# Four pairs' down rows stored plainly and added later, weight tails stored once, and the second half's operands prepared one name a gap

## The chip, the cores and the metric

The kernel runs on one core of a Trainium2 chip. Its time is the device time of one execution in microseconds (us). Times below come from three runs and from one further execution that was taken with the hardware profiler. The engines are TensorE (PE; PEld is its weight load), VectorE (DVE), ScalarE (ACT), GpSimd (POOL) and SyncE (SP, which here only issues DMAs). Sixteen DMA engines move the data of all queues.

## The reference

```python
x = A_x                                             # (1, 2048, 576); B_x is drawn too, but not read here
g = sigmoid((x * gate_w).sum(-1, keepdims=True))
a = irfft2(rfft2(x, axes=(-2, -1)) * (w_r + 1j * w_i), s=(2048, 576), axes=(-2, -1))
h = gelu(x @ w_gate, tanh approximation) * (x @ w_up)   # 576 -> 4608
b = h @ w_down                                      # 4608 -> 576
return g * a + (1 - g) * b
```

All is float32. The kernel splits an operand of a matmul into a high and a low part and adds the products of high with high, low with high and high with low, so one logical matmul is three or more.

## The kernel before

**Tiling.** The 2048 tokens are two halves of 1024 (p = 0, 1), the 4608 hidden features 36 tiles of 128, taken in 18 pairs i. The first two pairs of the first half are done in `normal`; all other work comes in 34 groups `(p, i)`: pairs 2 to 17 of the first half, then 0 to 17 of the second. A group is one call of `products`.

**A group.** Gate and up products of a group are formed from seven products of sums and differences of blocks (the names a11, a12, s2, s3, s1, a22, s4). Each product is `seven`, called for two column halves: six 128x512 matmuls on the 512 main features and a seventh (L1367) on the *tail*. The tail is the 32 features a half has left over. Its operand has 128 rows: on the weight side the high part of the 32 rows twice and the rest twice, on the x side high, rest, high, rest, so that one matmul forms all four cross products. Between the products stand the matmuls of `down` for earlier groups (L963): they multiply by `w_down` into a PSUM tile `pdn`, ACT drains it to one of four `stg` buffers (L995), and `put` sends `stg` to the DRAM buffer `yd[u]` of its 128 tokens, u = 0 to 15: the first time plainly from SP, later with an accumulating DMA from POOL (L976).

**Weight tails.** The tails of a pair's weights are worked out once, from the input `wt`, by `tail_piece`, ten times: `load` (L1242), `total` (four subtractions, L1246), `high` (a copy), `rest` (L1253) and `store` to the DRAM buffer `tails_d` (L1260). The first two pieces run before the first group, the other eight in the first groups, each spread over gaps 1 to 11 of every 12. They work in `wtb`: `raw_t` its first 896 columns, `high_t` its last 896. Before each product, `prep` loads its tail from DRAM into a weight slot (L1344), a DMA of 128 KB, three products ahead. There are four slots.

**What sets the order.** The program is written out in order by Python code. A *gap* is a point between matmuls at which `gap()` issues what is due: functions put there by `at(n, fn)`, n gaps ahead, and then steps of generators as long as their `credit` lasts, which grows with PE's work. The engines run their own instructions strictly in that order; SP and POOL queue DMAs in that order, and an instruction that waits holds all behind it on its engine.

**The spectral part** runs as such a generator beside the products, mostly on DVE and ACT: row transforms of each half of the tokens, then `columns` (column products on PE, L349, whose frequency-dependent factors come by DMA from POOL and SP), the inverse, and `adds`, which adds the result into `yd` by accumulating DMAs from POOL (L710). `inverse_rows(0)` and `(1)` do that for the two halves. In the last group `load_last` loads `yd[8..15]` back (L1017) for the last down rows.

**The second half's operands.** `other_operands` runs in the first half's groups near their end. It takes blocks of x of the second half (three at a time in `quads`), forms sums, and for each of seven names a high and a low part, which it stores to `kept_*` in DRAM (L1181, L1174). At the turn from the first to the second half, `swap` loads them.

The tail's load and store before, and the tail operand's copy:

```python
d = tails_d[n].rearrange("(r q p) k -> q r p k", r=4, q=4)          # prep, L1343
nc.sync.dma_start(f(w[:, 512:768]), d[q, :, :, 256 * m:256 * (m + 1)])
for r, x in enumerate((f(high_t), f(high_t), raw_t, raw_t)):         # store, L1259
    nc.sync.dma_start(d[r, 0:w, n % 2], x[0:w])
for q in (0, 64):                                                    # tail_of, L1053
    copy(o[q:q + 32], x[q:q + 32])
```

Of the kernel before, what the change touches and what calls it, by code (L numbers as in the profile page):

```python
# [10 lines left out]
F32 = mybir.dt.float32  # L11
# [4 lines left out]
P = 128  # L16
# [143 lines left out]
def _build(nc, tc, a):  # L160
    with ExitStack() as ctx:
# [34 lines left out]
        def set_tmp():  # L196
# [18 lines left out]
        tails_d = [dram.tile([4 * P, 7 * 256], F32, name=f"tails{i}", tag=f"tails{i}") for i in range(len(PAIRS))]  # L215
        yd = [dram.tile([P, D], F32, name=f"yd{i}", tag=f"yd{i}") for i in range(NB)]

        def ps_gu():
# [69 lines left out]
        def columns():  # L288
# [129 lines left out]
            for kb in range(16):  # L418
                was, more = kb > 0, kb + 1 < 16
                v = product(0, kb, xh, xl)  # L420
                if was:
                    copy(yh, vs)
                yield from step()
                copy(zr, v[:, 1, :NK])
                copy(t0, v[:, 0, :NK])
                yield from step()
                if was:
                    vec.tensor_tensor(yl, vs, f(yh), ALU.subtract)
                vec.tensor_tensor(zi, t0, zr, ALU.subtract)
# [24 lines left out]
                yield from waits(STEP - 7)  # L454
# [203 lines left out]
        def inverse_rows(h):  # L658
# [93 lines left out]
        added = {}  # L752
        aux = []
        later = []
        gens = []
        side = []
        credit = [0.0]
# [13 lines left out]
            later.sort(key=lambda x: x[0])  # L771

        def gap():

            count[0] += 1
            while later and later[0][0] <= count[0]:
                later.pop(0)[1]()
            if aux:
                aux.pop(0)()
            credit[0] = min(credit[0], cap[0])  # L780
            if not gens:
                return
            ahead = side and ops.get("ahead")
            while ahead and credit[0] > 0:
                v = next(side[0], None)
                if v is None:
                    break
                credit[0] -= v
            while credit[0] > 0:
                try:  # L790
                    v = next(gens[0])
                except StopIteration:
                    gens.pop(0)
                    v = None
                if v is None:
                    while side and not ahead and credit[0] > 0:
                        v = next(side[0], None)
                        if v is None:
                            break
                        credit[0] -= v  # L800
                    return
                credit[0] -= v
# [161 lines left out]
                          start=part == 0 and n == 0, stop=part == 1 and n == 2)  # L964
            tick(6 * 0.131)

        def put(u, write, first):

            o = stg[dnn[0] % 4].rearrange("p c k -> p (c k)")
            dnn[0] += 1  # L970
            added[u] = count[0]
            write(o)
            if first:
                nc.sync.dma_start(yd[u], o)
            else:
                pl.dma_start(yd[u], o, accum_op=ALU.add)  # L976

        def down(prev, t):
# [12 lines left out]
                copy(held(u).rearrange("p (c k) -> p c k", c=2), v[:, :, 0:HD])  # L991
            else:
                assert ops.get('released', 0) > min(dnn[0], 3)
                n = 1 if ops.get("late") else 0
                at(n, lambda: put(u, lambda o: act.activation(o.rearrange("p (c k) -> p c k", c=2), v[:, :, 0:HD], AF.Copy,  # L995
                                                              scale=omg[:, u:u + 1]), i == 0))
            behind[0] = t % 2 == 0
            gap()
            behind[0] = False
# [47 lines left out]
        def tail_of(o, x):  # L1047
# [98 lines left out]
        def other_operands():  # L1146
# [6 lines left out]
                ring.append(ring.pop(0))  # L1153
                return ring[-1]

            def highs(names, i):
                q = quads[i]
                at_ = dict(a11=q[0], a12=q[1], a22=q[3], s1=q[3], s3=q[2], s2=q[0], s4=q[1])
                out = []
                for n in names:  # L1160
                    out.append((n, i, at_[n], place()))
                    copy(fr(out[-1][3]), out[-1][2])
                return out

            def rests(items):
                for n, i, x, h in items:
                    o = h if i == 2 else x if n[0] == "s" else place()
                    vec.tensor_tensor(fr(o), x, h, ALU.subtract)
                    if i == 2:
                        def turn(h=h, x=x):  # L1170
                            for q in (0, 64):
                                copy(fr(h[q:q + 32]), x[q:q + 32])
                        at(1, turn)
                        at(2, lambda n=n, h=h: nc.sync.dma_start(kept[n][:, 2048:], h))  # L1174
                        yield 0.72
                        yield None
                        continue
                    else:
                        def store(n=n, i=i, h=h, o=o):
                            for c, s in ((0, h), (1, o)):  # L1180
                                nc.sync.dma_start(kept[n][:, 1024 * c + TB * i:1024 * c + TB * (i + 1)], s)  # L1181
                        at(2, store)
                    yield 0.72

            A, B = ("a11", "a12", "a22"), ("s1", "s3", "s2", "s4")

            def sums_of(i):
                yield from sums(quads[i] + quads[i][1:2])

            yield from waits(5)  # L1190
            load_xs(1, 2, quads[2])
            first = highs(A, 0)
            yield None
            for i in range(3):
                yield from rests(first)
                yield from sums_of(i)
                second = highs(B, i)
                if i < 2:
                    first = highs(A, i + 1)
                yield None  # L1200
                yield from rests(second)
                if i == 1:
                    at(5, ops.pop("go"))
            yield from waits(2)
            ops["kept"] = True

# [31 lines left out]
        def tail_piece(n, raw_t=raw_t, high_t=high_t):  # L1238
# [26 lines left out]
        class Block:  # L1265
# [58 lines left out]
            def prep(self, k, m, lead=0):  # L1324
# [49 lines left out]
        def products(b, k):  # L1374
# [295 lines left out]
```

## Time and profile before

| | |
|---|---|
| three runs | 1357.9, 1358.4, 1362.8 us; median 1358.4 |
| the profiled execution | 1358.5 us; its span, first to last instruction, 1356.7 us |
| busy share of the span | PE 97%, PEld 85%, DVE 84%, ACT 62%, POOL 21% |
| bytes moved by DMA | 274.6 MB, 203 GB/s over the span |

A span is what the profile covers; some 1.8 us lie outside it. Lines of the profile name engine, source line, operation and tiles as out<-in. "DMA share" is the mean busy share of the 16 DMA engines in a stretch. Where a tile has a number in the program (`til0`), the profile leaves it out.

### The profile page before, as it was taken

The numbers are of one execution on the slowest core, as the hardware profiler recorded it, in microseconds if no ns is written. First come the engines' busy times: TensorE is split into PE (matmuls) and PEld (weight loads), VectorE is DVE, ScalarE is ACT, GpSimd is POOL, SyncE is SP. The second block draws the span as 40 slices with busy tenths as digits, with TensorE's granted clock in tenths as the row PEclk, the third lists the DMA queues.
The fourth block names the chain that finished last, engine by engine and source line by source line (L and its number), as shares of the span: only waits on it lengthen the run. The fifth ranks groups of instructions, "written<-read, shape, count | busy, mean of one in ns | idle before, by whom it ended". The sixth has DMA issues, their size and how long they took to land.

```text
span 1356.7 us, 20505 instructions
## 1 busy us (share of the span) xinstructions
PE 1315.2 (97%) x7210; PEld 1157.2 (85%) x7210; DVE 1134.2 (84%) x1734; ACT 842.2 (62%) x1419; POOL 285.0 (21%) x360
## 2 busy tenths in 40 slices
PE   9999989999999998899979999999999999999998
PEld 7888878888888886788868888888888888888887
DVE  7888879988999985676958678867999977999974
ACT  5675645667565666767658777866656556556552
POOL 0011112221122111223422122221112223211232
PEclk9999999999999999999989999999999999999999
DMA  9779999897767799998998598887777789777799
GB/s 351 235 181 218 228 227 217 185 264 163 138 143 141 154 304 283 248 223 217 339 229 225 169 241 182 185 206 177 178 138 143 144 172 222 151 146 144 141 205 242
DMA packets 181103, 274.64 MB, mean 202 GB/s; under 512 B 14792, under 2 KB 95304, under 8 KB 180104
## 3 DMA queue, kind: packets, MB, share of 16 engines
q0 software_dynamic: 50000, 100.69, 44.5%
q1 hardware_dynamic: 130568, 172.21, 39.6%
q8 instruction: 56, 0.92, 0.3%
q10 hardware_dynamic: 432, 0.44, 0.1%
q14 instruction: 47, 0.39, 0.1%
HBM read 148.44 MB, written 126.61 MB: 203 GB/s over the span
## 4 chain that ended last, share of the span: by engine, by line
PE 66%; DMA 13%; issue 9%; ACT 4%; DVE 4%; POOL 2%; SPq 1%; DVEq 0%; POOLq 0%; ACTq 0%
PE pdn L963 22%; PE pgu L1365 17%; PE px L1365 16%; PE pgu L1367 3%; PE px L1367 3%; DMA tails<-wtb 2%; DMA gub<-tails 2%; POOL yd L976 2%; PE pdn L349 2%; DMA slot<-tails 1%; DMA wtb<-wt 1%; DMA gub<-ws 1%; ACT til L234 1%; ACT stg L995 1%; DMA kept_a<-wtb 1%
## 5 line engine op out<-in xcount | busy, mean ns | idle before, releaser
L976 POOL DMA_DIRECT2D yd<-stg x264 | 228.6, 870 | 1010.7 <-ACT stg L995 950.6
L995 ACT ACTIVATE stg<-pdn,omg 128x576 f32<-128x576 f32 x276 | 203.8, 740 | 292.4 <-PE pdn L963 186.9
L963 PE MATMUL pdn<-dn,hb 128*128 128x288 f32 x1356 | 201.1, 295 | 7.0 <-ACT stg L995 6.5
L963 PEld LDWEIGHTS pdn<-dn,hb 128*128 128x128 f32 x1356 | 192.1, 188 | 16.7 <-ACT stg L995 8.2
L1365 PE MATMUL pgu<-xhi,gub 128*128 128x512 f32 x480 | 150.3, 394 | 0.6 <-DVE gl L1391 0.4
L1365 PE MATMUL pgu<-til,gub 128*128 128x512 f32 x516 | 132.9, 392 | 2.7 <-ACT xraw L234 2.3
L963 PEld LDWEIGHTS pdn<-dn,ext 128*128 128x128 f32 x816 | 123.7, 190 | 10.6 <-DVE low L1028 0.5
L234 ACT ACTIVATE gub<-low 128x512 fp32r<-128x512 f32 (+1 forms) x163 | 100.8, 620 | 50.9 <-DVE low L1337 45.5
L963 PE MATMUL pdn<-dn,ext 128*128 128x288 f32 x816 | 130.8, 296 | 0.3 <-DVE low L1028 0.3
L963 PE MATMUL pdn<-dn,gub 128*128 128x288 f32 x816 | 129.7, 295 | 0.0
L1352 DVE TENSOR_TENSOR gub<-low,gub 128x512 fp32r<-128x512 f32 x151 | 103.5, 685 | 15.4 <-ACT gub L234 13.8
L963 PEld LDWEIGHTS pdn<-dn,gub 128*128 128x128 f32 x816 | 115.9, 189 | 0.0
L1365 PEld LDWEIGHTS pgu<-til,gub 128*128 128x128 f32 x516 | 94.0, 188 | 22.3 <-ACT xraw L234 3.8
L1365 PE MATMUL px<-xhi,gub 128*128 128x512 f32 x344 | 107.7, 394 | 3.0 <-ACT pgu L234 3.0
L1365 PE MATMUL px<-til,gub 128*128 128x512 f32 x396 | 102.7, 395 | 0.5 <-ACT xraw L234 0.5
L1365 PEld LDWEIGHTS pgu<-xhi,gub 128*128 128x128 f32 x480 | 86.8, 189 | 16.1 <-DVE gl L1391 1.3
L1365 PE MATMUL pgu<-xlo,gub 128*128 128x512 f32 x240 | 94.1, 392 | 0.0
L1365 PEld LDWEIGHTS px<-til,gub 128*128 128x128 f32 x396 | 73.1, 190 | 14.8 <-ACT xraw L234 1.1
L1365 PEld LDWEIGHTS px<-xhi,gub 128*128 128x128 f32 x344 | 62.2, 189 | 14.2 <-ACT pgu L234 3.7
L963 PE MATMUL pdn<-dn,hx 128*128 128x288 f32 x444 | 70.3, 294 | 0.0
L1337 DVE TENSOR_TENSOR low<-low 128x512 f32<-128x512 f32 x98 | 67.3, 687 | 1.6 <-DMA low<-ws 0.7
L1365 PE MATMUL px<-xlo,gub 128*128 128x512 f32 x172 | 67.6, 393 | 0.0
(301 smaller groups left out, 2728.0 us busy)
## 6 DMA issues: line engine op xcount, KB each, us to landing
yd<-stg POOLq DMA_DIRECT2D x264, 288.0 KB, 6.4
low<-ws SPq DMA_DIRECT2D x114, 256.0 KB
gub<-tails SPq DMA_DIRECT2D x179, 128.0 KB
gub<-wd SPq DMA_DIRECT2D x68, 288.0 KB
tails<-wtb SPq DMA_DIRECT2D x28, 448.0 KB
slot<-tails SPq DMA_DIRECT2D x59, 128.0 KB
gub<-ws SPq DMA_DIRECT2D x22, 256.0 KB
rows<-away SPq DMA_DIRECT2D x32, 145.0 KB
```

The source lines that it names most:

```text
L234: act.activation(o, i, AF.Copy)
L349: pe.matmul(v[:, al, :NK], cc[d][2 * al + q], two(x)[:, al], start=n == 0, stop=n == 2)
L963: pe.matmul(ps[half], h[:, l, c], d[:, q, half * HD:(half + 1) * HD], start=part == 0 and n == 0, stop=part == 1 and n == 2)
L976: pl.dma_start(yd[u], o, accum_op=ALU.add)
L995: at(n, lambda: put(u, lambda o: act.activation(o.rearrange("p (c k) -> p c k", c=2), v[:, :, 0:HD], AF.Copy, scale=omg[:, u:u + 1]), i == 0))
L1337: vec.tensor_tensor(o, p, q, ALU.subtract)
L1352: vec.tensor_tensor(v[:, 0:5:4], x, f(v[:, 1:4:2]), ALU.subtract)
L1365: pe.matmul(ps, l, x[:, t], start=first and t == 0 and q == 0, stop=False, skip_group_check=True)
L1367: pe.matmul(ps, w[:, 512 + P * s:512 + P * (s + 1)], xt, start=False, stop=True, skip_group_check=True)
```

## The change

1. **Down rows.** For pairs 13, 14, 16 and 17 of the first half, `put` sends `stg` plainly to a DRAM buffer of its own, `ye[i, u]`, issued by ACT: 32 stores. In `inverse_rows(0)` 32 accumulating DMAs from POOL, one each four gaps, add `ye` into `yd` from DRAM to DRAM. In the column stage (`ops["ahead"]`) the drain of `pdn` is issued after the other work of its gap (`post`).
2. **Weight tails.** High part and rest are stored once each, as interleaved rows, in a DRAM buffer half as large; the load names the 64 rows of a pair twice, by a broadcast over a new outer dimension of 2. On the x side the tail has each high row twice and then each low row twice, so its copy is one of 64 partitions. The eight pieces of the first groups alternate between `free_low` and `wtb` as `raw_t`, load four gaps before their block of twelve and store at gap 10 of it.
3. **Second half's operands.** `other_operands` makes one name a gap, with the rest of a name issued beside the next one's high part and its stores one DMA a gap; the loads of the third block are spread over four gaps. Column steps wait three gaps more at kb = 3 (`HOLD`).

In the diff, `dealt` is the former body of `gap`, `settle` issues the `rest` of the name before, and the loop over `B` is as that over `A`; `other_operands` copies its tails as `tail_of` does.

```diff
+HOLD = 3
+APART = (13, 14, 16, 17)
...
-        tails_d = [dram.tile([4 * P, 7 * 256], ...) for i in range(len(PAIRS))]
+        tails_d = [dram.tile([2 * P, 7 * 256], ...) for i in range(len(PAIRS))]
+        ye = {(i, u): dram.tile([P, D], F32, ...) for i in APART for u in range(8)}
...
@@ columns @@
+                    if kb == 3:
+                        yield from waits(HOLD)
...
@@ inverse_rows, h == 0 @@
+                for n, (i, u) in enumerate(ye):
+                    at(4 + 4 * n, lambda i=i, u=u: pl.dma_start(yd[u], ye[i, u], accum_op=ALU.add, max_dma_last_dim=D))
...
@@ gap @@
+            dealt()
+            while post:
+                post.pop(0)()
...
@@ put @@
             if first:
                 nc.sync.dma_start(yd[u], o)
+            elif (i, u) in ye:
+                act.dma_start(ye[i, u], o)
             else:
                 pl.dma_start(yd[u], o, accum_op=ALU.add)
...
@@ down @@
+                if ops.get("ahead"):
+                    post.append(out)
+                else:
+                    out()
...
@@ tail_of @@
-            for q in (0, 64):
-                copy(o[q:q + 32], x[q:q + 32])
+            copy(o[0:64], x[0:64])
...
@@ other_operands @@
+            def rest(n, i, x, h):
+                o = h if i == 2 else x if n[0] == "s" else place()
+                vec.tensor_tensor(fr(o), x, h, ALU.subtract)
...
+                    for c, s in ((0, h), (1, o)):
+                        at(2 + c, lambda c=c, s=s: nc.sync.dma_start(kept[n][:, 1024 * c + TB * i:...], s))
...
-            yield from waits(5)
-            load_xs(1, 2, quads[2])
+            yield from waits(3)
+            for q, x in enumerate(quads[2]):
+                at(7 + q, lambda q=q, x=x: nc.sync.dma_start(x, a["xs"][1, q // 2, q % 2][:, 2]))
...
+                for n in A:
+                    made = high(n, i)
+                    settle()
+                    pending.append(made)
+                    yield None
...
@@ tail_piece.store @@
-                d = tails_d[n // 2].rearrange("(r p) (m c k) -> r p c m k", r=4, m=7, c=2)
+                d = tails_d[n // 2].rearrange("(p r) (m c k) -> r p c m k", r=2, m=7, c=2)
-                for r, x in enumerate((f(high_t), f(high_t), raw_t, raw_t)):
+                for r, x in enumerate((f(high_t), raw_t)):
...
@@ prep.tail @@
-                    d = tails_d[n].rearrange("(r q p) k -> q r p k", r=4, q=4)
-                    nc.sync.dma_start(f(w[:, 512:768]), d[q, :, :, 256 * m:256 * (m + 1)])
+                    d = tails_d[n].rearrange("(q p) k -> q p k", q=4)[q, :, 256 * m:256 * (m + 1)]
+                    nc.sync.dma_start(f(w[:, 512:768]), d[None].to_broadcast([2, 64, 256]))
...
@@ products, opening group @@
+                at(6, lambda: credit.__setitem__(0, credit[0] - 2.0))
                 for q in range(2 * len(PAIRS) - 2):
-                    for n, fn in zip((1, 6, 8, 9, 11), tail_piece(q + 2)):
-                        at(n + 12 * q, fn)
+                    t = (free_low[:, 0:7 * P] if q % 2 == 0 else wtb[:, 0:7 * P]).rearrange("p (m k) -> p m k", m=7)
+                    for n, fn in zip((-4, 6, 8, 9, 10), tail_piece(q + 2, t)):
+                        at(max(1, n + 12 * q), fn)
...
@@ kernel @@
-    half = ... [np.arange(512, 544) + 32 * h] * 4
+    half = ... [np.repeat(np.arange(512, 544) + 32 * h, 2)] * 2
```

How the change stands in the engines' order, at three places. First SP in the first groups, from the store of the third tail piece to that of the fourth. `tails` are the DRAM buffers, `wt` the input, `gub` and `slot` the weight slots, `ws` and `wd` weights. Before:

```order
L1260 DMA tails1_107<-wtb_88 896x1x128 x4
L1344 DMA gub1_72<-tails0_106 128x1x256
L1242 DMA wtb_88<-wt 128x256
L1242 DMA wtb_88<-wt 128x2x128
L1344 DMA gub1_72<-tails0_106 128x1x256
L1319 DMA gub0_796<-wd 128x576 x2
L1310 DMA low_76<-ws 128x512 x2
L1344 DMA gub2_73<-tails0_106 128x1x256
L1344 DMA slot_74<-tails0_106 128x1x256
L1260 DMA tails1_107<-wtb_88 896x1x128 x4
```

After (the lines of the file have moved: L1288 is the store, L1372 the tail load, L1270 the load of `wt`):

```order
L1288 DMA tails1_107<-wtb_88 128x7x128
L1288 DMA tails1_107<-low_76 128x7x128
L1372 DMA slot_74<-tails0_106 128x1x256
L1372 DMA gub1_72<-tails0_106 128x1x256 x2
L1347 DMA gub0_818<-wd 128x576 x2
L1338 DMA low_76<-ws 128x512 x2
L1372 DMA gub2_73<-tails0_106 128x1x256
L1270 DMA low_76<-wt 128x256
L1270 DMA low_76<-wt 128x2x128
L1372 DMA slot_74<-tails0_106 128x1x256
L1288 DMA tails1_107<-wtb_88 128x7x128 x2
```

A piece is two stores instead of four, and it comes from two places (`low` is `free_low`). The tail loads stand in the same number between; each is still written as 128 rows of 256, and what has changed in it, the source, is only in the diff.

Second ACT, where the rows of pair 13 are first drained. Before:

```order
L1395 ACTIVATE gl0_81<-pgu_4546 128x512
L234 ACTIVATE xraw_83<-px0_4548 128x512
L234 ACTIVATE gub1_72<-low_76 128x2x256
L234 ACTIVATE xraw_83<-px1_4549 128x512
L995 ACTIVATE stg0_84<-pdn_4672,omg_92 128x576
L234 ACTIVATE hb0_78<-gl0_81 128x512
```

After (L1010 is the drain, L990 the DMA, L237 a copy):

```order
L1425 ACTIVATE gl0_81<-pgu_4550 128x512
L237 ACTIVATE tmp_89<-rows_94 128x512
L237 ACTIVATE wtb_88<-rows_94 128x512
L237 ACTIVATE xraw_83<-px0_4552 128x512
L237 ACTIVATE gub1_72<-low_76 128x2x256
L237 ACTIVATE xraw_83<-px1_4553 128x512
L1010 ACTIVATE stg0_84<-pdn_4678,omg_92 128x576
L990 DMA ye13_4_115<-stg0_84 128x576
L237 ACTIVATE hb0_78<-gl0_81 128x512
```

Behind the drain ACT itself issues the store, ahead of the copy into `hb`; copies of `other_operands` stand at other places.

Third POOL at the end of the program: L976 (L992 after) adds a drained `stg` into `yd`, L710 (L717 after) a spectral row. Before:

```order
L710 DMA yd11_122<-low_76 128x576
L976 DMA yd8_119<-stg0_84 128x576
L710 DMA yd12_123<-tmp_8271 128x576
L976 DMA yd9_120<-stg1_85 128x576
L710 DMA yd13_124<-tmp_8271 128x576
L710 DMA yd14_125<-tmp_8271 128x576
L976 DMA yd10_121<-stg2_86 128x576
L976 DMA yd11_122<-stg3_87 128x576
```

After:

```order
L717 DMA yd12_155<-wtb_88 128x576
L992 DMA yd10_153<-stg2_86 128x576
L992 DMA yd11_154<-stg3_87 128x576
L717 DMA yd13_156<-low_76 128x576
L717 DMA yd14_157<-low_76 128x576
L717 DMA yd15_158<-tmp_8380 128x576
L717 DMA yd8_151<-tmp_8380 128x576
L717 DMA yd9_152<-tmp_8380 128x576
```

Five spectral adds now stand behind the last add of a `stg` buffer, where before all stood ahead of it. Further ahead on POOL, the 32 adds from `ye` stand between the `stg` adds of the second half's groups, about two for each three of these.

More of the change, by code (lines that the diff above doesn't have):

```diff
@@ L214, in _build @@
                 for n in ("a11", "a12", "s2", "s3", "s1", "a22", "s4")}
-        tails_d = [dram.tile([4 * P, 7 * 256], F32, name=f"tails{i}", tag=f"tails{i}") for i in range(len(PAIRS))]
+        tails_d = [dram.tile([2 * P, 7 * 256], F32, name=f"tails{i}", tag=f"tails{i}") for i in range(len(PAIRS))]
+        ye = {(i, u): dram.tile([P, D], F32, name=f"ye{i}_{u}", tag=f"ye{i}_{u}") for i in APART for u in range(8)}
         yd = [dram.tile([P, D], F32, name=f"yd{i}", tag=f"yd{i}") for i in range(NB)]
@@ L965, in down_mm, with put @@
             tick(6 * 0.131)
-        def put(u, write, first):
+        def put(u, write, first, i=None):
             o = stg[dnn[0] % 4].rearrange("p c k -> p (c k)")
@@ L993, in down @@
                 assert ops.get('released', 0) > min(dnn[0], 3)
-                n = 1 if ops.get("late") else 0
-                at(n, lambda: put(u, lambda o: act.activation(o.rearrange("p (c k) -> p c k", c=2), v[:, :, 0:HD], AF.Copy,
-                                                              scale=omg[:, u:u + 1]), i == 0))
+                out = lambda: put(u, lambda o: act.activation(o.rearrange("p (c k) -> p c k", c=2), v[:, :, 0:HD], AF.Copy,
+                                                              scale=omg[:, u:u + 1]), i == 0, i)
+                if ops.get("ahead"):
+                    post.append(out)
+                else:
+                    out()
             behind[0] = t % 2 == 0
@@ L1154, in place, with high @@
                 return ring[-1]
-            def highs(names, i):
+            def high(n, i):
                 q = quads[i]
[L1158 to L1168, printed above, removed]
-                    if i == 2:
[L1170 to L1175, printed above, removed]
-                        yield None
[L1177 to L1183, printed above, removed]
@@ L1185, in other_operands @@
-            A, B = ("a11", "a12", "a22"), ("s1", "s3", "s2", "s4")
-            def sums_of(i):
-                yield from sums(quads[i] + quads[i][1:2])
-            yield from waits(5)
-            load_xs(1, 2, quads[2])
[L1192 to L1201, printed above, removed]
+                x = dict(a11=q[0], a12=q[1], a22=q[3], s1=q[3], s3=q[2], s2=q[0], s4=q[1])[n]
@@ new lines, in high, with turn @@
+                h = place()
+                copy(fr(h), x)
+                return n, i, x, h
+            def rest(n, i, x, h):
+                o = h if i == 2 else x if n[0] == "s" else place()
+                vec.tensor_tensor(fr(o), x, h, ALU.subtract)
+                credit[0] -= 0.72
+                if i == 2:
+                    def turn():
+                        copy(fr(h[0:64]), x[0:64])
+                    at(1, turn)
+                    at(3, lambda: nc.sync.dma_start(kept[n][:, 2048:], h))
+                else:
+                    for c, s in ((0, h), (1, o)):
+                        at(2 + c, lambda c=c, s=s: nc.sync.dma_start(kept[n][:, 1024 * c + TB * i:1024 * c + TB * (i + 1)], s))
@@ new lines, in other_operands, with settle @@
+            yield from waits(3)
+            for q, x in enumerate(quads[2]):
+                at(7 + q, lambda q=q, x=x: nc.sync.dma_start(x, a["xs"][1, q // 2, q % 2][:, 2]))
+            A, B = ("a11", "a12", "a22"), ("s1", "s3", "s2", "s4")
+            pending = []
+            def settle():
+                if pending:
+                    rest(*pending.pop(0))
+            for i in range(3):
+                for n in A:
[3 more added lines that the diff above has]
+                    yield None
+                    if i == 2:
+                        yield None
+                settle()
+                if i == 2:
+                    yield None
+                a11, a12, a21, a22 = quads[i]
+                for k, (o, x, z, op) in enumerate(((a22, a21, a22, ALU.add), (a21, a11, a21, ALU.subtract),
+                                                   (a11, a22, a11, ALU.subtract), (a12, a12, a11, ALU.subtract))):
+                    vec.tensor_tensor(o, x, z, op)
+                    credit[0] -= 0.72
+                    if k % 2:
+                        yield None
+                for n in B:
+                    made = high(n, i)
+                    settle()
+                    pending.append(made)
+                    yield None
+                    if i == 2:
+                        yield None
@@ L1632 @@
     wdp = wd.reshape(NT, P, D)[:, :, col]
-    half = np.stack([np.concatenate([np.arange(256) + 256 * h] + [np.arange(512, 544) + 32 * h] * 4) for h in range(2)])
+    half = np.stack([np.concatenate([np.arange(256) + 256 * h] + [np.repeat(np.arange(512, 544) + 32 * h, 2)] * 2) for h in range(2)])
     mid = half[:, 0:256]
```

5 lines of the change are left out of this document (4 added, 1 removed).

## The prediction

> **What bounds the kernel now.** I read the busy shares first, then who waits for whom, then the DMA queues and their issues, and at last short stretches in which one kind of transfer runs alone.
>
> ```profile
> PE 1315.2 (97%) x7210; PEld 1157.2 (85%) x7210; DVE 1134.2 (84%) x1734; ACT 842.2 (62%) x1419; POOL 285.0 (21%) x360
> ...
> core 0: 1356.7 us, clock 0.992
> ```
>
> PE is the bound: 1315.2 us of a span of 1356.7, at 0.992 of its clock. All that a change can win is the idle 41.5 us and the 0.8% of clock (10.9 us). The waits of PE on landings of weight tails, and the two largest on ACT, are:
>
> ```profile
> PEld px L1367 <- DMA gub<-tails: 6.8, 4, 3.5
> ...
> PE pdn L963 <- ACT stg L995: 6.5, 7, 2.0
> ...
> PE px L1367 <- DMA slot<-tails: 6.2, 1, 6.2
> ...
> PE px L1367 <- DMA gub<-tails: 5.4, 3, 3.1
> ...
> PE pgu L1367 <- DMA gub<-tails: 4.2, 1, 4.2
> ...
> PE px L1365 <- ACT pgu L234: 3.0, 2, 2.5
> ```
>
> Columns: engine, tile and line, who ended the wait; us in total, times, longest. The three PE rows on tails make 6.2 + 5.4 + 4.2 = 15.8 us: where PE waits, it mostly waits for a DMA that is late. (PEld's row is the same waits seen by the weight loads.) So the second resource to look at is the DMA engines. The bytes by queue, and the issues that the change touches:
>
> ```profile
> q0 software_dynamic: 50000, 100.69, 44.5%
> q1 hardware_dynamic: 130568, 172.21, 39.6%
> ...
> yd<-stg POOLq DMA_DIRECT2D x264, 288.0 KB, 6.4
> ...
> gub<-tails SPq DMA_DIRECT2D x179, 128.0 KB
> ...
> tails<-wtb SPq DMA_DIRECT2D x28, 448.0 KB
> slot<-tails SPq DMA_DIRECT2D x59, 128.0 KB
> ...
> yd<-wtb POOLq DMA_DIRECT2D x9, 288.0 KB, 9.0
> ...
> tails<-slot SPq DMA_DIRECT2D x4, 448.0 KB
> tails<-wtb SPq DMA_DIRECT2D x8, 224.0 KB
> ...
> yd<-low POOLq DMA_DIRECT2D x4, 288.0 KB, 8.3
> ...
> yd<-tmp POOLq DMA_DIRECT2D x3, 288.0 KB, 8.6
> ```
>
> There are 179 + 59 = 238 loads of a weight tail, 7 for each of 34 groups, 31.2 MB. The next rows are stretches (busy us of PE, PEld, DVE, ACT, POOL; then clock, DMA share of 16 engines, GB/s). The first has only tail loads in flight, the second only wide loads, the third and fourth accumulates into `yd` at their fastest and slowest; then a quiet group and two crowded ones; then the first three 25 us.
>
> ```profile
> 1185.30:1186.80 1.50, 1.50 (x8) 1.27 (x7) 1.50 (x2) 0.00 (x0) 0.85 (x1) 1.00 0.27 96
> 11.00:12.50 1.50, 1.50 (x8) 1.25 (x7) 1.40 (x4) 1.50 (x4) 0.00 (x0) 1.00 1.05 402
> 1130.25:1131.75 1.50, 1.50 (x7) 1.22 (x8) 1.50 (x3) 1.45 (x3) 0.35 (x1) 1.00 1.14 211
> 241.50:243.00 1.50, 1.50 (x11) 1.36 (x11) 1.50 (x3) 0.55 (x1) 0.00 (x0) 1.00 1.06 136
> 394.80:429.80 35.00, 35.00 (x195) 31.02 (x194) 34.34 (x43) 18.23 (x31) 6.80 (x8) 1.00 0.73 142
> 626.30:666.80 40.50, 38.30 (x214) 33.46 (x213) 30.63 (x49) 28.66 (x50) 17.85 (x29) 1.00 1.02 300
> 626.30:666.80 40.50, 6.46 (x8) 1.00 1.02 300
> 104.80:141.10 36.30, 35.32 (x195) 30.97 (x194) 30.71 (x52) 18.77 (x32) 5.95 (x7) 1.00 0.97 235
> 0.00:25.00 25.00, 23.55 (x91) 18.94 (x92) 17.87 (x34) 14.88 (x31) 3.13 (x10) 1.00 0.93 338
> 25.00:50.00 25.00, 25.00 (x140) 22.20 (x139) 23.61 (x40) 13.40 (x22) 0.00 (x0) 1.00 0.70 250
> 50.00:75.00 25.00, 24.78 (x137) 21.71 (x136) 17.64 (x29) 20.77 (x35) 0.97 (x2) 1.00 0.82 234
> ```
>
> The row that decides: a tail load alone moves 96 GB/s at a share of 0.27, while wide loads move 402 at 1.05. Packets overlap a little (shares pass 1), so 0.27 is four of sixteen engines, at 24 GB/s each, as in the wide load (402/16 = 25). The source of a tail load is four blocks of 32 rows; a wide load has 128 rows on both sides. So the number of engines follows the outermost count of the source, here 4. One load holds each of its four engines 131072 B / 96 GB/s = 1.37 us.
>
> **The tail loads after the change.** The source becomes `d[None].to_broadcast([2, 64, 256])`: outermost count 2. By the same pattern I expect two engines, each held 2.73 us a load, 7 x 2.73 = 19.1 us a group in place of 9.6 on four. I assume that they are the same engines each time; no view names them.
>
> The Trainium skill, "DMA: Bandwidth & Descriptors", section "Rules for kernel authors", says the same of this case: an outermost dim of under 16, "e.g. a leading zero-stride broadcast of c copies", confines the whole DMA to at most c engines; its section "Why a DMA increments its semaphore by 16 and not by 1" adds that DMAs issued from SP take the lowest-numbered engines. The trace agrees as far as it goes (0.27 for a source of 4). Its table gives ~27 GiB/s for an engine, 29 GB/s; at that an estimate of the tail loads would be 31.2 MB / 2 / 29 = 538 us a run instead of the 650 below; the row's 24 decides.
>
> What else do those two engines carry? Prices for one of 16 engines: wide traffic 400 GB/s (row 2). An accumulate of 294,912 B: 1.40 us at 211 GB/s, 2.17 us at 136.
> - Quiet group: 142 GB/s x 35.0 us = 4.97 MB; 8 accumulates 2.36 MB, tails 0.92 MB, rest 1.69 MB. 8 x 1.40 + 1.69/400 = 15.4 us; with tails 25.0 of 35.0 us now, 34.5 after: just full.
> - Busiest group: 300 x 40.5 = 12.15 MB; 8 accumulates (POOL x8 on `yd`), rest 8.87 MB. 11.2 + 22.2 + 9.6 = 43.0 us now on the four engines, in 40.5 us. They are the bound there already. After: 52.5.
> - Crowded group at 104.8: 8.53 MB, 7 accumulates: 9.8 + 13.9 + 9.6 = 33.3 in 36.3 us; after 42.8.
>
> In the full groups the sum at low prices lies between 6% above and 9% below the group's length, so I take low prices, with 2% for gaps in the queue.
>
> Whole run on the two engines: q1 without tails (172.2 - 31.2)/400 = 352 us; 280 accumulates (264 + 9 + 4 + 3) x 1.40 = 391; rest of q0, 18.1 MB, 45; tails 238 x 2.73 = 650. Sum 1439 us, at the slow accumulates 1655. That is above PE's 1315: the two engines become the bound.
>
> **The other parts.**
> - Tail stores halved: 32 x 448 + 8 x 224 KB = 16.5 MB, half saved: -21 us of each engine's time. SP's wait for them (L1242 in the rows below) goes too. On the path only as engine time.
> - 32 accumulates become plain stores: 32 x (1.40 - 0.74) = -21 us of engine time; added later from DRAM, 32 x 1.40 = +45 us (at the slow price 69). No DRAM-to-DRAM add is in the trace; I take the SBUF row, since either way a destination is read and written, and 1.40 to 2.17 as bounds. Net with the stores +3: 1442 us.
> - These adds fall in about six groups of PE time that are quiet now, some 5 each: 34.5 + 7 to 42 us.
> - POOL issues them between the accumulates, two of each three; a row takes 0.85 us and POOL is 79% idle. Even at four times that (512 pieces against 128) a drain queued behind one waits 3.4 us, and the quiet group has 35.0/8 = 4.4 us a drain and four `stg` buffers. Zero.
> - ACT issues the 32 plain stores at 0.6 us each (row below): 19 us over four pairs, ACT busy 28.7 of 40.5 us. What waits behind each is the next copy of `hb`. Zero while DMA is the bound.
> - Pairs of 32-partition copies become one of 64: 14 copies fewer on ACT, which is 62% busy. Off the path.
> - Drains after the gap's copies in the column stage: later by a copy or two; PE's wait of 6.5 us on `stg` bounds what the old order cost. Zero.
> - One name a gap: stores no longer stand six in a row ahead of tail loads on SP. A gain only if the loads are otherwise in time.
> - The spectral part ends later: HOLD and the new order push the adds of `yd13,14,15,8,9` behind the last drain. Now:
>
> ```profile
> SPq L1242 <- DMA tails<-wtb: 25.6, 7, 5.9
> 1350.49 1.19 ACTq L1030 DMA_DIRECT2D y<-stg  x2
> ...
> 1327.90 2.28 POOL L710 DMA_DIRECT2D yd<-tmp  x2
> ...
> 1333.74 0.86 POOL L976 DMA_DIRECT2D yd<-stg  x1 [0.72 <-ACT stg L995]
> ...
> 1326.34 7.33 DMA yd<-tmp
> ...
> 1333.73 7.67 DMA low<-yd
> ```
>
> The last drain issues at 1333.7 and ends at 1334.6. Five adds at 1.14 us follow: the last is issued near 1340, lands 8.6 us later, and its reload takes some 5 to 7.7 us: 1354 to 1356, while ACT now sends the finished `stg` at 1350.5. With the last add on DVE behind it that is +4 to +9, or 0 if PE is late anyway; I take +8.
>
> **Sum.** 1442 x 1.02 = 1471; + 14 us in which the engines have no work at the start (25 x (0.07 + 0.30 + 0.18)); + 8 at the end; + 1.8 outside the span (1358.5 against 1356.7). That is 1495 us. The profiled execution's 1358.5 is the median of the three runs, 1358.4. Bounds of the two-engine case: 1442 x 0.94 + 24 = 1379 (price 6% too high, as in the busiest group) and 1657 + 24 = 1681 (slow accumulates everywhere); I keep 1415 to 1600, nearer the low price because the full groups stand there.
>
> **Rivals.**
> - Faster: the loads keep four or more engines, or take changing pairs, so that no engine is full. Then the waits above go: 15.8 + 6.5 + 3.0 us, and up to 10.9 of clock, 36 us at most; I take two thirds, 23, less 8 at the end: 1344 us. It decides if a lone tail load shows a share of 0.27 or more. Against it: the source's 4 gave four. 12%.
> - No change: two engines, but the work on them fits, as the quiet group's 34.5 of 35.0 would allow. The crowded groups speak against it (42.8 and 52.5 us). About 1358 us, 3%.
> - Worse: accumulates at their slow price on full engines, 1681 us. The busiest group at that price would need 8 x 2.17 + 22.2 + 9.6 = 49.2 us and took 40.5. 6%.
>
> **Chances.** My case 79%. Range 1415 to 1600 leaves out the faster case (12%), the worse (6%) and little else. A measurement here tells 0.5% (6.8 us) from nothing. Faster 0.12, within 0.5% 0.03, slower 0.85.
>
> **What would show it.** A stretch with lone tail loads at a share near 0.13 and 48 GB/s; PE waits on `gub<-tails` and `slot<-tails` of over 100 us in sum, spread over nearly all groups; the group now at 626 near 47 us (52.5 less 8 x 0.66 for plain stores), the one at 104 near 39 (42.8 less two halved pieces of 2.1), the quiet ones at 35 to 37, those with DRAM adds near 42; mean DMA share lower, since 14 engines idle. Wrong if the lone load keeps 0.27, or if groups stay at 35 us with 0.13.

## The result, and the profile after

| | runs | median | profiled span | clock |
|---|---|---|---|---|
| before | 1357.9 to 1362.8 us | 1359.4 us | 1356.7 us | 0.992 |
| after | 1542.2 to 1545.4 us | 1544.0 us | 1542.4 us | 0.947 |

Medians here are of four executions each, the profiled one among them. The changed kernel takes 1.135 times as long (95% interval 1.133 to 1.138), 184.6 us more. The forecast was 1495 us, in a range of 1415 to 1600. The first rows are after's busy shares and span, the second its waits of PE on weight tails.

```profile
PE 1370.5 (89%) x7210; PEld 1189.5 (77%) x7210; DVE 1138.3 (74%) x1734; ACT 834.5 (54%) x1405; POOL 291.3 (19%) x360
...
core 0: 1542.4 us, clock 0.947
```

```profile
PE pgu L1395 <- DMA gub<-tails: 48.4, 17, 7.4
...
PE px L1395 <- DMA slot<-tails: 33.8, 9, 6.1
PE px L1395 <- DMA gub<-tails: 30.0, 11, 8.6
```

PE's idle time went from 41.5 to 171.9 us, and the same 7210 matmuls were busy for 55 us more, at a mean granted clock of 0.947 in place of 0.992. In the whole groups below, and in the last stretch, the clock is 1.00 where PE never stands and 0.80 to 0.96 where it stands for 3.8 to 18.2 us. The three rows of direct waits on tails make 112.2 us (before 15.8); a fourth has 1.1 us. They fall in 20 of the 34 groups. So the list of waits shows less than two thirds of the 184.6 us: the rest stands in other waits and in the clock.

Queues, after (packets, MB, share of 16 engines), and then stretches (a group is taken from its first tail matmul to that of the next group): one within a quiet group, a whole quiet group, the groups that before had at 104.8 and 626.3, two groups with DRAM adds, and the last stretch.

```profile
q0 software_dynamic: 62288, 100.69, 41.0%
q1 hardware_dynamic: 113644, 163.95, 32.6%
```

```profile
1449.20:1450.90 1.70, 1.70 (x9) 1.42 (x8) 1.63 (x4) 1.35 (x3) 0.86 (x1) 1.00 0.14 33
421.30:456.30 35.00, 35.00 (x195) 31.02 (x194) 34.33 (x43) 18.22 (x31) 6.80 (x9) 1.00 0.69 137
102.20:143.30 41.10, 37.32 (x195) 32.23 (x194) 33.51 (x58) 20.26 (x34) 6.77 (x9) 0.96 0.76 171
677.30:730.00 52.70, 41.71 (x213) 36.09 (x212) 30.60 (x48) 28.10 (x46) 17.10 (x30) 0.87 0.86 271
1207.10:1253.60 46.50, 37.68 (x196) 31.86 (x194) 32.64 (x52) 18.46 (x32) 11.58 (x12) 0.93 0.80 141
1253.60:1314.00 60.40, 43.20 (x196) 36.23 (x196) 30.68 (x49) 24.21 (x36) 19.51 (x21) 0.80 0.86 166
1470.80:1542.40 71.60, 53.43 (x309) 48.15 (x307) 37.09 (x58) 19.72 (x32) 17.24 (x19) 0.90 0.82 196
```

The first row is the sign-post: a share of 0.14 is two of sixteen engines, and such stretches of 0.7 to 2.7 us come back several times in the two quiet groups that I read this way. They move 33 GB/s, not the 48 that two engines have with tail loads alone: 15 to 19 GB/s an engine is between a tail load's 24 and an accumulate's 13 (211/16). The trace's packet records show why: in the first row's stretch they are 27 pieces of tail loads (1024 B) and 12 of accumulates (2304 B), nothing else. The two engines still work off their shares of the accumulates, after the other fourteen have run dry. Seven groups stay at 35.0 us, all of them 35.0 before; 22 of the 34 are longer than before by more than 0.5 us, one by 24 us, and two are shorter.

### The profile page after: what moved, and what is told of

Same layout as the page of the kernel before. It is cut to its first block, busy times and chain, and to the rows that moved or that the text cites. A ratio compares the mean times of both kernels' runs of the same rounds, so it can differ in the third digit from the quotient of the medians.

```text
span 1542.4 us, 20477 instructions
## 1 busy us (share of the span) xinstructions
PE 1370.5 (89%) x7210; PEld 1189.5 (77%) x7210; DVE 1138.3 (74%) x1734; ACT 834.5 (54%) x1405; POOL 291.3 (19%) x360
## 3 DMA queue, kind: packets, MB, share of 16 engines
q0 software_dynamic: 62288, 100.69, 41.0%
## 4 chain that ended last, share of the span: by engine, by line
PE 44%; DMA 31%; issue 13%; POOL 4%; ACT 4%; DVE 3%; SPq 2%; ACTq 0%; DVEq 0%; POOLq 0%
PE pdn L977 15%; DMA gub<-tails 13%; PE pgu L1393 11%; PE px L1393 10%; DMA slot<-tails 7%; POOL yd L992 3%; DMA rows<-away 3%; PE px L1395 2%; PE pgu L1395 2%; DMA rows<-xs 1%; DMA wtb<-wf 1%; DMA kept_s<-xtl 1%; PE pdn L352 1%; DMA gub<-wd 1%; DMA yd<-wtb 1%
## 5 line engine op out<-in xcount | busy, mean ns | idle before, releaser
L1010 ACT ACTIVATE stg<-pdn,omg 128x576 f32<-128x576 f32 x276 | 204.5, 741 | 347.5 <-PE pdn L977 223.7
L992 POOL DMA_DIRECT2D yd<-stg x232 | 212.4, 939 | 795.7 <-ACT stg L1010 758.9
L1393 PE MATMUL pgu<-xhi,gub 128*128 128x512 f32 x480 | 154.2, 403 | 13.9 <-ACT px L237 9.7
L977 PEld LDWEIGHTS pdn<-dn,ext 128*128 128x128 f32 x816 | 130.5, 200 | 22.1 <-DVE low L1047 7.2
L977 PE MATMUL pdn<-dn,ext 128*128 128x288 f32 x816 | 136.9, 305 | 9.5 <-DVE low L1047 6.8
L1393 PE MATMUL pgu<-til,gub 128*128 128x512 f32 x516 | 139.3, 407 | 2.7 <-ACT xraw L237 2.7
L1393 PE MATMUL px<-xhi,gub 128*128 128x512 f32 x344 | 111.7, 407 | 19.4 <-ACT xraw L237 12.5
L237 ACT ACTIVATE gub<-low 128x512 fp32r<-128x512 f32 (+1 forms) x163 | 100.8, 620 | 45.2 <-DVE low L1365 37.8
L977 PEld LDWEIGHTS pdn<-dn,gub 128*128 128x128 f32 x816 | 119.5, 194 | 0.0
L1393 PEld LDWEIGHTS pgu<-til,gub 128*128 128x128 f32 x516 | 99.0, 197 | 22.3 <-ACT xraw L237 3.2
L1395 PE MATMUL pgu<-til,gub 128*128 128x512 f32 x172 | 73.0, 425 | 48.4 <-DMA gub<-tails 48.4
L1393 PE MATMUL px<-til,gub 128*128 128x512 f32 x396 | 105.8, 404 | 0.0
L1395 PEld LDWEIGHTS pgu<-til,gub 128*128 128x128 f32 x172 | 34.4, 200 | 62.7 <-DMA gub<-tails 56.0
```

Source lines behind the costliest of these rows:

```text
L237: act.activation(o, i, AF.Copy)
L977: pe.matmul(ps[half], h[:, l, c], d[:, q, half * HD:(half + 1) * HD], start=part == 0 and n == 0, stop=part == 1 and n == 2)
L1010: out = lambda: put(u, lambda o: act.activation(o.rearrange("p (c k) -> p c k", c=2), v[:, :, 0:HD], AF.Copy, scale=omg[:, u:u + 1]), i == ...
L1393: pe.matmul(ps, l, x[:, t], start=first and t == 0 and q == 0, stop=False, skip_group_check=True)
L1395: pe.matmul(ps, w[:, 512 + P * s:512 + P * (s + 1)], xt, start=False, stop=True, skip_group_check=True)
```

## The experiments

**1. One part alone, and one part undone.** Four kernels do this. The first is before with loads of outermost count 2:

```diff
# e1_before_two, on before
-  nc.sync.dma_start(f(w[:, 512:768]), d[q, :, :, 256 * m:256 * (m + 1)])
+  for c in (0, 2):
+      nc.sync.dma_start(f(w[32 * c:32 * c + 64, 512:768]), d[q, c:c + 2, :, 256 * m:256 * (m + 1)])
```

> The kernel before, with one edit: each tail load becomes two loads of two blocks of 32 rows each (source outermost count 2 in place of 4), the same 128 rows and 128 KB in all. Theory (two engines carry all tail loads and become the bound): a lone pair of loads shows a share near 0.13 and 48 GB/s, the time comes out at 1475 to 1520 us with the waits of PE on tails above 100 us. Rival (the count of engines is not what costs; the DRAM adds, ACT's issues or the new order cost the 185 us): 1355 to 1370 us, waits on tails under 30 us.

Measured 1523.6 us against 1360.0 for before: +163.6 us, ratio 1.120 (1.118 to 1.122), 4 us over the theory's range. PE waits for the tails again, 136.3 us with a fourth row of 2.2 us:

```profile
PE pgu L1368 <- DMA gub<-tails: 86.6, 21, 13.7
PE px L1368 <- DMA gub<-tails: 34.5, 7, 8.9
PE px L1368 <- DMA slot<-tails: 13.0, 5, 5.7
```

The expected pair of loads at 48 GB/s does not appear alone. A stretch in a quiet group again has the share of two engines, at 27 GB/s, and its records are 15 tail pieces and 10 of accumulates:

```profile
503.40:504.80 1.40, 1.40 (x8) 1.17 (x7) 1.36 (x4) 1.38 (x3) 0.85 (x1) 1.00 0.13 27
```

The count of two alone makes most of the loss. The reverse edit, on after:

```diff
# e2_after_wide, on after
-  nc.sync.dma_start(f(w[:, 512:768]), d[None].to_broadcast([2, 64, 256]))
+  for c in (0, 64):
+      nc.sync.dma_start(f(w[c:c + 64, 512:768]), d)
```

> The kernel after, with one edit: each tail load becomes two loads of 64 plain rows (outermost count 64), one for each half of the slot's partitions, in place of one load with an outermost broadcast of 2. Theory: 16 engines share each load, the waits of PE on tails fall under 20 us, and the time is 1330 to 1360 us; what is left over 1358 is the end of the spectral part (up to 9 us). Rival (the DRAM adds or the new order cost most): 1400 us or more.

Measured 1332.6 us, ratio to before 0.980 (0.978 to 0.982): 211 us below after, and faster than before. No wait of PE on a tail is left among its rows; the largest is the reload at the end:

```profile
PE pdn L977 <- DVE low L1047: 7.7, 1, 7.7
```

So after holds a gain that the load buried. Does before suffer from its four engines already? Its load as four of 32 rows:

```diff
# e3_before_wide, on before
+  for c in range(4):
+      nc.sync.dma_start(f(w[32 * c:32 * c + 32, 512:768]), d[q, c, :, 256 * m:256 * (m + 1)])
```

> The kernel before, with one edit: each tail load becomes four loads of 32 plain rows, which 16 engines share if the outermost count decides. Theory (four engines were already full in the crowded groups): 15.8 us of waits on tails mostly go and some of the lost clock with them, 1325 to 1345 us. Rival (the waits of before come from landing latency or from queues, not from four full engines; or 714 more issues on SP cost): 1355 us or more.

Measured 1352.6 us, ratio 0.995 (0.992 to 0.997): between the two. The group at 626 stays at 40.5 us and those at 104 to 220 at 36 to 44, and waits on tails of 11.0 us remain. Four engines cost before some 7 us, not the 15 or more that the theory wanted. In these first groups the sums of the next weight tails wait for their load, as this row of the waits from 100 to 190 us shows:

```profile
DVE wtb L1246 <- DMA wtb<-wt: 8.2, 2, 6.3
```

The last of the four is after with `APART = ()`, two engines kept:

> The kernel after without its first part: no pair goes plainly to DRAM buffers, all of these 32 rows are added into yd directly from stg, and there are no DRAM-to-DRAM adds. Tail loads stay on two engines. Theory (two engines are the bound, and the DRAM adds put 32 x 2.0 = 64 us on them less 21 for the plain rows): 1480 to 1505 us, and groups 23 to 29, which took 44 to 60 us, take 38 to 45. Rival A (the DRAM adds are the main cost): under 1420 us. Rival B (they cost nothing): 1535 us or more.

Measured 1503.1 us, ratio 1.104 (1.102 to 1.107), inside the theory's range. The groups with DRAM adds, 44 to 60 us in after, are at 35.0 to 47.8, where the theory had 38 to 45. Two of them in e4, which take 44.5 and 60.4 us in after:

```profile
1129.80:1164.80 35.00, 35.00 (x196) 31.02 (x195) 34.86 (x44) 18.86 (x32) 7.65 (x10) 1.00 0.67 134
1235.60:1283.40 47.80, 38.07 (x195) 31.86 (x194) 24.46 (x40) 22.38 (x35) 13.02 (x15) 0.93 0.82 168
```

The plain rows and their adds cost 40.9 us on full engines. e4 is 20.6 us faster than e1. The third part gives no sign of its own here (e11 below), so this is what the second part wins beside its load: the stores saved, the second buffer and the earlier loads of the pieces, which no run takes apart.

**2. What after's other parts do when no engine is full.**

e5 is e2 with `APART = ()`:

> The kernel after with the tail loads on 16 engines (as e2), and without its first part: no plain rows, no adds from DRAM to DRAM. With two engines full that part cost 41 us. Theory (it costs engine time and nothing else, so with no engine full it costs under 5 us either way): 1328 to 1338 us. Rival (it is what brings e2 its 20 us over e3, by relieving the crowded groups 12 to 15): 1345 to 1352 us.

Measured 1330.3 us (0.978, 0.976 to 0.981). The rows and adds that cost 41 us on two full engines cost 2 us here, less than can be told.

e6 is e2 with `HOLD = 0`:

> The kernel e2 with HOLD = 0: the column steps no longer wait three gaps at kb = 3. Theory (e2's last stretch, from the start of the last group, takes 63.5 us where before took 54.8, since the last accumulates end later and PE waits 7.7 us for the reload behind them; three gaps are some 5 us): 1325 to 1329 us, PE's wait at the end 1 to 4 us. Rival (the place of the last accumulates follows the drains, or the column steps lose elsewhere what they win): 1331 us or more.

Measured 1332.9 us (0.980, 0.978 to 0.982), and PE's waits for the reload are 8.2 us in two, the longer 6.5. My reason for the late end was wrong: without HOLD the last accumulates stand no earlier on POOL; e9 below shows what moves them.

e7 goes back to two engines and asks why a DRAM add was dearer than an accumulate. Before the change q0 had 50000 packets, after 62288, 384 more for each of 32 adds: 512 pieces of 576 B where an accumulate has 128 of 2304 B.

```diff
# e7_after_rows, on after
-  pl.dma_start(yd[u], ye[i, u], accum_op=ALU.add, max_dma_last_dim=D)
+  pl.dma_start(yd[u], ye[i, u], accum_op=ALU.add, max_dma_last_dim=4 * D)
```

> The kernel after (tail loads on two engines) with one edit: each of the 32 adds from DRAM to DRAM moves 128 pieces of 2304 B in place of 512 of 576 B. After, such an add held an engine for some 2.2 us (32 pieces at 69 ns) and the first part of the change cost 41 us in all (after against e4). Theory (the pieces are what made the add dearer than the 1.40 us of an accumulate from SBUF): 8 pieces of 175 to 200 ns, 1.4 to 1.6 us an add, so the time falls by 32 x 0.6 to 0.8 = 20 to 25 us, to 1519 to 1525 us. Rival (read and write in DRAM are what costs, whatever the piece): 8 pieces of 275 ns, 1544 us as it was.

Measured 1530.6 us (1.125, 1.122 to 1.128), 13.4 us below after: more than the rival's nothing, less than the theory's 20 to 25. The pieces are a part of the price. By time, with the prediction's 21 us for the rows made plain, an add costs (40.9 + 21)/32 = 1.93 us in after and, against e4, (27.5 + 21)/32 = 1.52 us here: an estimate by which the theory was right on e7 and had after's add too dear at 2.2. Its queue row has the old count:

```profile
q0 software_dynamic: 50000, 100.69, 40.0%
```

e8 is before with the second part of the change alone, and e2's loads:

> The kernel before with the second part of the change alone (tails stored once, two buffers, the copies of 64 partitions), and its loads on 16 engines by two plain loads of 64 rows. Theory (halved stores and the second buffer take the waits out of the first groups, where e3 stays at 36 to 44 us in groups 1 to 4 and e2 is at 35.0): 1335 to 1343 us, groups 1 to 4 at 35 to 37. Rival (e2's gain over e3 comes from the operands made one name a gap or from the plain rows): 1348 to 1353 us.

Measured 1326.5 us, ratio 0.975 (0.973 to 0.978), better than expected and better than e2. A stretch of a quiet group, the first crowded group, the group that before had at 626, and the last stretch of e8; then the last stretch of e2:

```profile
387.20:388.20 1.00, 1.00 (x6) 0.81 (x6) 1.00 (x2) 0.46 (x1) 0.63 (x1) 1.00 0.01 4
...
102.10:137.10 35.00, 35.00 (x195) 31.03 (x194) 32.44 (x56) 20.39 (x34) 6.82 (x9) 1.00 0.90 213
604.10:644.60 40.50, 38.30 (x214) 33.46 (x213) 30.64 (x49) 28.68 (x49) 17.63 (x29) 1.00 1.02 302
...
1271.50:1325.20 53.70, 49.77 (x309) 45.72 (x307) 29.30 (x44) 19.78 (x32) 19.00 (x19) 1.00 0.97 236
```

```profile
1265.40:1328.90 63.50, 51.85 (x309) 47.37 (x307) 36.40 (x56) 19.70 (x32) 17.13 (x19) 0.95 0.88 200
```

Where after had the tails of two engines at 0.14, e8 has nothing in flight (0.01). Its groups 1 to 4 take 35.0 us each. The group at 604 still takes 40.5 us with 16 engines, at a share of 1.02 for all of them: that group is full of bytes, not of tails. And e2 loses 9.8 us on e8 in the last stretch.

**3. The end, the best version, and the second part as it was written.**

e9 is e5 with the old `other_operands` as a whole (its tail copies of 64 partitions kept):

> The kernel e5 (tail loads on 16 engines, no plain rows and DRAM adds) with the operands of the second half made in the old order. In e6 the last accumulates of the spectral result stood in the same place of POOL's queue as in e2, from the 7050th to the 7113th matmul; before has them from the 6974th to the 7062nd, and with the old order of the operands they stand there again. Theory (the order of the operands, not HOLD, makes the end late): the stretch from the last group on falls from e5's 63.6 to 54 us, PE's wait on the reload of 6 us goes, the time is 1316 to 1323 us. Rival (something else than the place of these accumulates makes the end late): 1328 us or more.

Measured 1320.7 us, ratio 0.971 (0.968 to 0.974): the fastest of all. Its last stretch, and its largest waits of PE:

```profile
1262.60:1316.30 53.70, 49.80 (x309) 45.74 (x308) 29.25 (x44) 19.79 (x32) 18.18 (x19) 1.00 0.98 242
```

```profile
PE pdn L352 <- DMA tmp<-col: 2.9, 1, 2.9
PE px L1383 <- ACT pgu L237: 2.5, 1, 2.5
```

The last stretch is 53.7 us again and the wait for the reload is gone: the new `other_operands` made the end late. PE is busy 99% of this span. e9 differs from e8 only in HOLD and the drains' place, and is 5.8 us faster; their ratios' intervals (0.968 to 0.974 and 0.973 to 0.978) touch, so that these two win anything is not shown.

e10 is e9 with the plain rows and DRAM adds:

> The kernel e9 with the plain rows and the DRAM adds of the first part kept. Theory (with no engine full they cost a few us in the two groups where the adds stand closest, 42.0 and 37.8 us in e2 against 36.1 and 35.0 in e5, and win some in the crowded groups): 1316 to 1326 us. Rival (they also press on the reload at the end): 1330 us or more.

Measured 1329.7 us (0.978, 0.974 to 0.981), 9 us over e9 and between the two. Three rows of three of its wait lists (POOL, ACT, PE):

```profile
POOL yd L717 <- DMA yd<-ye: 6.4, 1, 6.4
```

```profile
ACT wtb L714 <- DMA yd<-wtb: 17.3, 2, 13.9
```

```profile
PE pdn L977 <- ACT stg L1010: 10.4, 2, 9.5
```

ACT stands 13.9 us until an accumulate of the spectral result has landed and frees its buffer, a drain of `pdn` stands behind that on ACT, and PE waits 9.5 us. The group in which this falls takes 46.6 us (35.5 in e9). That accumulate took 10.6 us from issue to landing, where the first one of e9 took 5.9, with the DMA share at 1.00 meanwhile. POOL's wait, for a `yd[u]` that a DRAM add was still writing, comes after its issue and holds the accumulate behind it. That this is the whole 9 us is read from the trace, not tried by itself; e2, with the adds in another place against the operands, lost only 2 us on e5.

e11 is e8 with the load as in the change:

> The kernel before with the second part of the change alone, as it was written: the tails stored once and loaded by one broadcast over an outermost dimension of 2. It differs from e8 in the load alone. Theory (the load's two engines are the whole loss): 1495 to 1508 us, near e4, some 175 us over e8. Rival (the loss needs the other parts as well): under 1450 us.

Measured 1502.6 us (1.104, 1.100 to 1.108): 176 us over e8 for that one line. It equals e4, so the operands' order, the drains' place and HOLD together come to nothing while two engines are full.

## Why the prediction was right, and where its sizes were off

**The load's engines: right.** Share 0.14, PE waits of 112 us, and e1, e2 and e11 undo or make the loss with the load alone. PE's waits were over 100 us, as forecast, but in 20 groups, not nearly all. The Trainium skill, "DMA: Bandwidth & Descriptors", section "Why a DMA increments its semaphore by 16 and not by 1", says that a DMA uses the largest number of engines up to 16 that divides both sides' slowest dims, and from SP the lowest-numbered ones; the counts agree with the shares here, 0.27 for 4, 0.14 for 2 and 1.05 for a wide load on 16. Which engines they are no row names. That they are the same each time is read from the sign-post: while only two engines were busy, they had tail pieces and left-over pieces of accumulates at once. With changing pairs the left-overs would lie on all engines, no group would have been full, and the sum below would not fit.

**The price of work on full engines: right.** The prediction's sum, made for after's own groups with GB/s x length, 1.40 us an accumulate, 400 GB/s for the rest and 19.1 us of tails:

- at 421.3: 4.80 MB, 8 accumulates, rest 1.52: 11.2 + 3.8 + 19.1 = 34.1; took 35.0.
- at 102.2: 7.03 MB, 8 accumulates, rest 3.75: 11.2 + 9.4 + 19.1 = 39.7; took 41.1 (forecast 39).
- at 677.3: 14.28 MB, 2 accumulates, rest 12.77: 2.8 + 31.9 + 19.1 = 53.8; took 52.7 (forecast 47, which gave each plain row 0.66 us less and had 12.15 MB in the group).

Over the whole run, by issues and bytes of each group, the two engines of e1 have 1444 us of work, of e4 and e11 1423 us: the 21 us that the halved stores were to save, and 20.6 measured. So close a fit is partly luck: the records have 16128 pieces of 512 B fewer at a median of 27 ns, which is 27 us an engine, and the second buffer is in the 20.6 too. Two small slips in the prediction move nothing: 33.3 us is 8% below 36.3, not 9, and two thirds of 36 us are 24, not 23.

**The DRAM adds: mis-sized.** "I take the SBUF row", 1.40 us, within 1.40 to 2.17. In the trace's packet records a 576-B piece takes a median of 69 ns; an engine has 32 of an add: 2.2 us, the upper bound. (By the same records an accumulate is 8 x 196 ns = 1.57 us, above its 1.40, since packets overlap; by time the estimate beside e7 is 1.93 us an add.) The groups speak for 2.2 more than for 1.40: at 1207.1, 6.56 MB with 7 accumulates and 5 adds (the row's x12 on POOL) need 9.8 + 11.0 + 5.3 + 19.1 = 45.2 us and took 46.5; at 1.40 the adds would give 41.2. At 1253.6, 15 accumulates and 6 adds need 60.6 us and took 60.4. The forecast there was 42. 32 x 0.8 = 26 us, most of the difference between 1442 us and after's 1472 us of work on the two engines. Net the first part cost 40.9 us, where the prediction had 45 - 21 = 24. That 2.2 lies at the bound of 2.17 is chance. The row at 241.5 us, read as accumulates at their slowest, holds 226 packets of 512 B, the size of the tail stores' pieces, and 38 of accumulates, so 136 GB/s is no price of an accumulate; 1655, 1681 and the worse rival rest on it alone.

**The idle of the full engines: too small.** After is 1542.4 us long for 1472 of work, so they idle 70 us: 15 in the first 77 us (forecast 14), 14 in the last 71.6, in which the work is 57, and some 41 between. The prediction had 2% (29 us) for the middle and 8 at the end. In e1 it is 79 us, where it would have been 43. What was left out: the groups in which PE is the bound leave the engines 0.5 to 1 us of their 35.0 each, and in the last stretch only 4 of the 238 tail loads are left, so that it runs on its own chain. The largest single parts, 7.7 and 4.9 us, fall in after's groups at 730.0 and 779.2. In the first, ACT waits for a load of `wd` that took 13.6 us to land, and PE behind ACT, as two of its waits show; what holds these groups was not tried.

```profile
ACT ext L237 <- DMA gub<-wd: 11.0, 1, 11.0
...
PE pgu L1393 <- ACT px L237: 8.8, 1, 8.8
```

With the adds this is 30 + 19 of the 49 us by which 1495 was low.

**The end of the spectral part: the size near, a reason wrong.** In wide loads the last stretch is 63.5 us against 53.7, +9.8 (bounds 4 to 9, or 0; taken 8), on the chain accumulate, reload, PE as forecast. "HOLD and the new order push the adds": HOLD does not (e6), the operands' order does (e9). With two engines full it cannot be told from the other idle time.

**POOL's and ACT's queues, "zero": right while DMA was the bound.** With no engine full the plain rows and their adds cost 2 us in e2 (against e5) and 9 in e10 (against e9). In e10 the cost comes through ACT, which stands for a late accumulate, and not through the two queue terms that the prediction priced.

**The faster rival** named the condition, not enough of the gain: with no engine full it gave 1344 us, and e2 takes 1332.6. It kept the crowded first groups (35 to 42 us before) as they were, but the halved stores and the second buffer, which I had "on the path only as engine time", take them to 35.0 us (e8).

## What to carry to other kernels

Look at the outermost dimension of every small, frequent DMA: a source of 2 blocks in place of 4 doubled what each load asked of its engines, and on two engines 238 loads of 128 KB cost 176 us more than on 16, though the mean DMA share was only 0.69 to 0.86 in the whole groups of after shown above. Mean shares hide this; a short stretch in which little else is in flight shows the number of engines as its share times 16 (0.27 and 0.14 here), and then the work of one such engine can be added up group by group. When a change of several parts is slower, undo the part that fills the resource before judging the others: after's second part is worth 2.5% once its load is spread, and its `other_operands` costs 10 us (e9 against e5) that could not be seen before.

## What the runs showed of the hardware

- What an accumulating DMA costs an engine depends on its pieces: in after's packet records 2304 B take a median of 196 ns accumulating and 93 ns plain, 576 B accumulating 69 ns. That is 11.8, 24.8 and 8.3 GB/s. Four small pieces (276 ns) cost 1.4 times one large one. The small ones come from DRAM and the large ones from SBUF; e7's adds from DRAM in pieces of 2304 B won 13.4 us on after's.
- More issues from SP showed no cost here: with four loads for one (e3, 714 more) PE's waits on tails fell from 15.8 to 11.0 us and the time by 7.4 us. What an issue costs by itself was not measured.
- PE's granted clock falls with its idle time: 0.992 before, 0.947 after and 0.999 in e9, with 41.5, 171.9 and 14.1 us idle, and the same matmuls are busy for 1315, 1370 and 1302 us.
